# Grouped-query decode attention: a shorter TensorE program, head and exp sums in one matmul, z built on GpSimd

## Chip, cores, metric

One core of a Trainium2 chip. The metric is the device time of one execution in microseconds (us), as the median of several; lower is better.

## The reference

Two tokens (B = 2, one position each) attend over a cache of 32768 positions, with 32 query heads on 8 key/value heads of width 128. A small gated MLP of the same input multiplies the result. Everything is bf16.

```python
def _A_ref(x, k_cache, v_cache, wq, wo):        # x [2,1,512], caches [2,8,32768,128]
    q = (x @ wq) ...                            # 32 heads, 4 to each K/V head
    scores = einsum("bhqd,bhkd->bhqk", q, k) * (Dh ** -0.5)
    p = softmax(scores)
    o = einsum("bhqk,bhkd->bhqd", p, v)
    return o.reshape(B, Sq, Hq * Dh) @ wo
xn = layernorm(x);  s = A(xn);  g = silu(B(xn)) # B: a small MLP, w1 to w4
return x + s * g
```

The caches are 2 x 8 x 32768 x 128 x 2 bytes each, 268.4 MB together, and every byte is used once. There are 16 groups, one for each pair of token and K/V head. Each brings 8.39 MB of K and 8.39 MB of V.

## The kernel before

K and V of a group are loaded by one DMA each. `kbuf` has three slots of half a K, so that the next K can be loaded once the first half of the present one is consumed. `vbuf` has room for one V. VectorE transposes K in 16 pieces into four T buffers. TensorE multiplies them with z (the query heads, shifted), ScalarE takes the exp, VectorE transposes the result to `pt`, and TensorE forms the product with V in `o`. A last step adds the four head slots of `o`, divides by the exp sums and stores the heads' values. Cut to what matters:

```python
# SP: the order of the loads, and what each waits for
for m in range(1, NG):
    sp.wait_ge(p_k, m);  load_k(m)       # first half of K(m-1) has been multiplied
    sp.wait_ge(p_o, m);  load_v(m)       # value product of m-1 is done
# ScalarE, each group
for j in range(4): act.copy(out=z[...], in_=qr[...])
for i in range(2):
    take(act, s_sc);  act.activation(eps_[i], sc[i], Exp, accum_out=rss[i])
take(act, s_o);  act.copy(out=ob, in_=o)
# VectorE, each group
heads(...)        # take(s_x); reciprocal of S; oT * rec * mask; reduce -> oA
for i in range(2):
    for r in range(8): take(s_tf);  dve.transpose(T[...], kbuf[...])
for i in range(2):                       # around each transpose of exp: sel * exp sums -> sms
    take(dve, s_e);  ...;  dve.transpose(pts[h], eps_[i]);  ...
# TensorE, each group
take(s_ob);  for t in range(4): pe.matmul(oT, lhsT=sel_o[t], rhs=ob[t])      # fp32
for i in range(2):
    for r in range(8): take(s_t);  4 matmuls z x T -> sc[i]
    mark(s_tf);  ...                     # 1x1 matmuls, only to raise a semaphore
take(s_p);  pe.matmul(S, lhsT=sms[1], rhs=ones_f[:, 0:1])
64 matmuls pts x vbuf -> o;  mark(p_o)
```

The softmax here doesn't subtract the row's maximum and nothing guards it: scores larger than these inputs give would overflow.

## Time and profile before

| | before |
|---|---|
| time, median of 3 runs | 654.21 us (654.19 to 655.46) |
| span of the profiled execution | 652.8 us |
| bytes read | 280.50 MB |
| TensorE, VectorE, ScalarE, GpSimd busy | 386.2, 346.0, 76.7, 7.7 us |
| TensorE matmul records | 2406 |

"Busy" is the time in which an engine executes. Against it stand the DMA queue's 99.4%, and the time from issue to landing of each load (a load has landed when its last bytes are in the buffer).

### The profile page before, as it was taken

The numbers are of one execution on the slowest core, as the hardware profiler recorded it, in microseconds if no ns is written. First come the engines' busy times: TensorE is split into PE (matmuls) and PEld (weight loads), VectorE is DVE, ScalarE is ACT, GpSimd is POOL, SyncE is SP. The second block draws the span as 40 slices with busy tenths as digits, with TensorE's granted clock in tenths as the row PEclk, the third lists the DMA queues.
The fourth block names the chain that finished last, engine by engine and source line by source line (L and its number), as shares of the span: only waits on it lengthen the run. The fifth ranks groups of instructions, "written<-read, shape, count | busy, mean of one in ns | idle before, by whom it ended". The sixth has DMA issues, their size and how long they took to land. (4 is left out here: it accounts for less than half of the span.)

```text
span 652.8 us, 6524 instructions
## 1 busy us (share of the span) xinstructions
PE 386.2 (59%) x2406; PEld 156.5 (24%) x2438; DVE 346.0 (53%) x412; ACT 76.7 (12%) x184; POOL 7.7 (1%) x29
## 2 busy tenths in 40 slices
PE   0548195672828658293764829367383945828785
PEld 0113132230313213131221213123121322212332
DVE  4257191753809266391835629174481926539570
ACT  1320102020010201101020010201001020010100
POOL 3100000000000000000000000000000000000000
PEclk9769688695978859697786878878697896869798
DMA  9999999999999999999999999999999999999997
GB/s 386 475 396 448 446 446 410 434 446 450 414 426 446 450 422 418 446 450 422 418 446 450 430 410 450 446 438 402 450 446 446 398 446 446 446 406 434 426 442 294
DMA packets 6506, 280.53 MB, mean 430 GB/s; under 512 B 736, under 2 KB 1000, under 8 KB 1256
## 3 DMA queue, kind: packets, MB, share of 16 engines
q1 hardware_dynamic: 6492, 280.50, 99.4%
q8 instruction: 1, 0.02, 0.0%
q10 hardware_dynamic: 12, 0.01, 0.0%
q14 instruction: 1, 0.01, 0.0%
HBM read 280.50 MB, written 0.00 MB: 430 GB/s over the span
## 5 line engine op out<-in xcount | busy, mean ns | idle before, releaser
L585 PE MATMUL bank<-T,z 128*128 128x512 bf16 x992 | 272.6, 422 | 189.7 <-PEq L46 184.9
L512 DVE STREAM_TRANSPOSE T<-kbuf 128x1024 int32<-128x1024 int32 x256 | 290.7, 1211 | 130.5 <-DVEq L46 130.5
L585 PEld LDWEIGHTS bank<-T,z 128*128 128x128 bf16 x1024 | 97.4, 103 | 352.1 <-issue 274.9
L602 PE MATMUL bank<-vbuf,pt 128*16 128x512 bf16 x1024 | 73.0, 449 | 2.5 <-PEq L46 2.5
L489 ACT ACTIVATE ep<-bank 128x512 bf16<-128x512 f32 x32 | 19.1, 598 | 438.5 <-ACTq L46 438.5
L533 DVE RECIPROCAL rec<-bank 128x1 f32<-128x1 f32 (+1 forms) x17 | 2.9, 169 | 118.8 <-DVEq L46 118.8
L602 PEld LDWEIGHTS bank<-vbuf,pt 128*16 128x16 bf16 x1024 | 27.6, 102 | 39.7 <-issue 21.5
L521 DVE STREAM_TRANSPOSE pt<-ep 128x512 bf16<-128x512 bf16 x32 | 22.9, 715 | 22.0 <-DVEq L46 22.0
L567 PE MATMUL bank<-ob,sel_o 128*128 128x128 f32 x136 | 19.7, 289 | 16.4 <-PEq L46 16.4
L595 PE MATMUL bank<-ones_f,sm 128*128 128x1 f32 x32 | 6.2, 264 | 31.3 <-PEq L46 31.3
L567 PEld LDWEIGHTS bank<-ob,sel_o 128*128 128x128 f32 x136 | 16.9, 196 | 21.8 <-issue 21.8
L493 ACT COPY ob<-bank 128x512 f32<-128x512 f32 x16 | 9.4, 587 | 102.6 <-ACTq L46 102.6
L482 ACT ACT_TABLE_LOAD x16 | 20.5, 1283 | 0.3
L595 PEld LDWEIGHTS bank<-ones_f,sm 128*128 128x128 f32 x32 | 5.3, 210 | 32.2 <-issue 32.2
L482 ACT COPY z<-qr 32x16 bf16 x64 | 13.0, 202 | 0.7
L451 PE MATMUL bank<-vbuf,h_bf 128*32 128x512 bf16 x14 | 4.9, 523 | 6.2 <-DVE h_bf L448 6.2
L562 PE MATMUL bank<-ident 128*1 128x1 bf16 x64 | 8.4, 165 | 0.0
L328 PE MATMUL bank<-ident,xn_bf 17*128 17x17 bf16 x4 | 0.3, 177 | 13.1 <-POOL x L319 13.1
L562 PEld LDWEIGHTS bank<-ident 128*1 128x1 bf16 x64 | 4.0, 82 | 16.2 <-issue 14.4
L541 DVE TENSOR_REDUCE oA<-xm 128x128 f32 x16 | 5.9, 366 | 3.8 <-DVEq L46 3.8
L535 DVE SCALAR_TENSOR_TENSOR xm<-bank,rec,mask 128x128 f32<-128x128 f32 (+1 forms) x17 | 6.0, 351 | 2.5 <-DVEq L46 0.2
L489 ACT ACTIVATION_READ_ACCUMULATOR ep<-bank 128x1 f32 x32 | 6.4, 200 | 0.2
(75 smaller groups left out, 55.1 us busy)
## 6 DMA issues: line engine op xcount, KB each, us to landing
vbuf<-in_A_v_cache_dram SPq DMA_DIRECT2D x4, 4096.0 KB, 29.5
kbuf<-in_A_k_cache_dram SPq DMA_DIRECT2D x2, 4096.0 KB, 22.9
kbuf<-in_A_wq_dram SPq DMA_DIRECT2D x1, 4096.0 KB, 13.5
vbuf<-in_B_w_dram SPq DMA_DIRECT2D x2, 1792.0 KB, 18.2
kbuf<-in_A_wo_dram SPq DMA_DIRECT2D x3, 1024.0 KB, 34.4
kbuf<-in_A_wo_dram SPq DMA_DIRECT2D x1, 512.0 KB, 37.1
kbuf<-in_A_wo_dram SPq DMA_DIRECT2D x1, 256.0 KB, 37.3
kbuf<-in_A_wo_dram SPq DMA_DIRECT2D x2, 128.0 KB, 37.1
```

Of the source, the lines that this page charges most:

```text
L482: i = act.copy(out=z[32 * j:32 * j + 32, :, :, c:c + rep], in_=qr[32 * j:32 * j + 32, :, :, bass.ds(m * rep, rep)],)
L489: act.activation(out=eps_[i][:, :], in_=sc[i][:, :], func=ACT.Exp, scale=inv_sqrt_dh, accum_out=rss[i][:, :]).then_inc(s_e, 1)
L493: act.copy(out=ob[:, :], in_=o[:, :]).then_inc(s_ob, 1)
L512: dve.transpose(out=Ts[(NR * i + r) % T_BUFS][:, :].rearrange("p (b t k) -> p t b k", b=NB, t=RT), in_=kt[:, r * W:(r + 1) * W].rearrange( ...
L521: dve.transpose(out=pts[h][:, :, :].rearrange("p r (t h) -> p t r h", h=rep), in_=eps_[i][:, :].rearrange("p (t r h) -> p t r h", r=NR, h= ...
L535: dve.scalar_tensor_tensor(out=xm[p0:, :, :], in0=oT[p0:, :].rearrange("p (w r) -> p w r", w=WL), scalar=rec[p0:, 0:1], in1=mask[p0:, :].u ...
L541: dve.tensor_reduce(out=dst, in_=xm[p0:, :, :].rearrange("p w r -> p r w"), axis=AX.X, op=ALU.add).then_inc(s_r, 1)
L562: pe.matmul(mark_ps, lhsT=ident[:, 0:1], rhs=ident[:, 0:1], start=True, stop=True).then_inc(sem, 1)
L567: mm = pe.matmul(oT, lhsT=sel_o[:, t, :, :, :].rearrange("p j h w -> p (j h w)"), rhs=ob[:, t * Dh:(t + 1) * Dh], start=(t == 0), stop=(t ...
L585: mm = pe.matmul(sc[i][:, :], lhsT=z[:, nb, e, zc:zc + 128], rhs=Tb[:, nb, :, e], start=(r == 0 and nb == 0 and e == 0), stop=(r == NR - 1 ...
L595: pe.matmul(S, lhsT=sms[1][:, :], rhs=ones_f[:, 0:1], start=True, stop=True)
L602: mm = pe.matmul(o[32 * j:32 * j + VT * rep, :], lhsT=pts[h][:, r, a * VT * rep:(a + 1) * VT * rep], rhs=vt[:, u * VT:(u + 1) * VT, :].rea ...
```

## The change

The intent is a TensorE program that is short (446 instructions, as the prediction has it) and less work around each group. The two halves of a group become a TensorE loop with register addresses, and the groups a loop with a counter. The four selection matmuls and the exp-sum matmul become one fp32 matmul of 129 columns. For this VectorE masks `o` and adds its four head slots, and writes the sum of the two exp sums into column 129. The marker matmuls go: ScalarE raises those semaphores, and V now waits for the heads. GpSimd builds z. The prologue is rearranged in the same spirit (transposes on VectorE, one memset of all of PSUM, the MLP's matmuls in loops). At the end, three quarters of the second half of wo also go through the packed product. Core of the diff, with cuts marked:

```diff
-        sp.wait_ge(p_o, m)
+        sp.wait_ge(s_r, m + 1)            # V after the heads of the group before
         load_v(m)
 ...
-    with act.Fori(0, NG) as m:            # z copies, two exps, copy of o
+    with act.Fori(0, NG):
         for i in range(NPART):
             take(act, s_sc)
+            act.sem_inc(s_tl, 1)
+            act.sem_inc(p_k, 1)
+            if i == NPART - 1:
+                act.sem_inc(s_zf, 1)
             act.activation(... Exp ..., accum_out=rss[i]).then_inc(s_e, 1)
-        take(act, s_o)
-        act.copy(out=ob[:, :], in_=o[:, :]).then_inc(s_ob, 1)
+    with pool.Fori(0, NG) as m:
+        take(pool, s_zf)
+        pool.tensor_tensor(out=zw, in0=qr[... m ...], in1=sel_j[...], op=ALU.mult).then_inc(s_z, 1)
 ...
     def heads(dst, p0):
+        take(dve, s_o)
+        then(dve.tensor_tensor(out=ox, in0=o, in1=sel_t (broadcast), op=ALU.mult))
+        dve.tensor_reduce(out=ob[:, 0:Dh], in_=ox as "p d t", op=ALU.add).then_inc(s_ob, 1)
         take(dve, s_x)
-        then(dve.reciprocal(out=rec[p0:, :], in_=S[p0:, :]))
+        then(dve.reciprocal(out=rec[p0:, :], in_=oT[p0:, Dh:]))
 ...
     def head_sums():
         take(pe, s_ob)
-        for t in range(VT):
-            mm = pe.matmul(oT, lhsT=sel_o[:, t, ...], rhs=ob[:, t * Dh:(t + 1) * Dh], ...)
+        mm = pe.matmul(oT, lhsT=sel_h[...], rhs=ob[:, :], start=True, stop=True)
 ...
-        for i in range(NPART):            # written out twice, marks after each
+    with pe.Fori(0, NPART) as i:
             ... pe.matmul(sc2[:, bass.ds(i * 512, 512)], lhsT=z[...], rhs=Tb[...])
-        pe.matmul(S, lhsT=sms[1][:, :], rhs=ones_f[:, 0:1], start=True, stop=True)
```

## The prediction

> **What bounds the kernel now.** I read the page first, for which unit never rests. The DMA row of the slices and the queue table answer it.
>
> ```profile
> DMA  9999999999999999999999999999999999999997
> q1 hardware_dynamic: 6492, 280.50, 99.4%
> q8 instruction: 1, 0.02, 0.0%
> HBM read 280.50 MB, written 0.00 MB: 430 GB/s over the span
> ```
>
> One queue keeps the 16 DMA engines busy for 99.4% of the span; TensorE stands at 59% and VectorE at 53%. So the question is only whether the change can open a hole in that stream, or lengthen what comes before its first byte or after its last. The fetch of instructions is one packet of 0.02 MB. The stretch table, cut into windows of 38.64 us (the distance between two K landings), shows whether the rate wanders. The columns are PE, PEld, DVE, ACT and POOL busy, clock, DMA share, GB/s:
>
> ```profile
> 80.14:118.78 38.64, 23.78 (x140) 9.40 (x142) 20.78 (x24) 4.17 (x10) 0.00 (x0) 0.81 1.00 434
> 311.98:350.62 38.64, 23.80 (x140) 9.45 (x142) 20.79 (x24) 4.18 (x10) 0.00 (x0) 0.81 1.00 434
> 543.82:582.46 38.64, 23.86 (x140) 9.54 (x142) 20.79 (x24) 4.17 (x10) 0.00 (x0) 0.81 1.00 434
> ```
>
> All of the 14 full groups run at 434 or 435 GB/s. A group brings K and V of 8.39 MB each, 16.78 MB, and 16.78 MB / 434 GB/s = 38.66 us: the period is the transfer and nothing else. The single slices of 396 to 450 on the page are whole packets falling on one or the other side of a border. Last, the chain that ended last, which tells what follows the stream:
>
> ```profile
> 613.16 36.97 DMA kbuf<-in_A_wo_dram
> 650.13 0.04 issue
> 650.18 0.26 PE bank L637 x4
> 650.46 0.30 DVE sg L662
> 650.79 0.29 DVE out L664
> ```
>
> The last bytes of wo land at 650.13 us, and only 0.95 us of work follows before the output's DMA is issued. Before the stream there is about 1 us (the first issue is at 0.00).
>
> How much delay can the stream take? A load is issued when its buffer is free, and waits behind the one in flight. The DMA issue view gives the time from issue to landing:
>
> ```profile
> kbuf<-in_A_k_cache_dram SPq DMA_DIRECT2D x15, 27.5
> vbuf<-in_A_v_cache_dram SPq DMA_DIRECT2D x14, 31.4
> ```
>
> A transfer takes 8.39 / 434 = 19.3 us, so a typical K load is issued 27.5 - 19.3 = 8.2 us early and a V load 31.4 - 19.3 = 12.1 us. About 1 us of each is the issue's own latency. That leaves 7 us and 11 us in hand, and all that the change does inside a group has to be held against them.
>
> **What the Trainium skill says.** "DMA: Bandwidth & Descriptors", section "Where 436 GB/s comes from", derives 435 GB/s from the 16 SBUF ports, and expects about 358 from the HBM side for a transfer like this one. The trace shows 434, so here the port figure is the one met, and the HBM figure is not the limit with this one core running. "Runtime: NRT & Kernel Launch", section "Instruction fetch mechanics", says that instructions come in blocks of 256 through a small buffer and that a taken branch out of the buffered window stalls. I take that for the intent of the 446-instruction program. The trace before shows one fetch packet on q8 in the whole span, so there is no stall of that kind to win back. "VectorE: DVE Perf Modes", section "The perf-mode tier table", puts a fp32 tensor_tensor and a tensor_reduce at the slowest mode whatever the memory, which I use for the two new VectorE operations. Before, a 128x128 reduction took 0.366 us and a 512-wide statistics pass 0.69 us, which agrees with about 1 ns per element plus a fixed part of some 0.2 us.
>
> **The change part by part, inside a group.** Tail of group 14 before, from the timeline:
>
> ```profile
> 570.94 0.59 ACT L493 COPY ob<-bank 128x512 f32<-128x512 f32 x1 [6.97 <-ACTq L46]
> 571.67 1.13 PE L567 MATMUL bank<-ob,sel_o 128*128 128x128 f32 x8 [0.86 <-PEq L46]
> 572.95 0.17 DVE L533 RECIPROCAL rec<-bank 128x1 f32<-128x1 f32 x1 [7.89 <-DVEq L46]
> 573.27 0.35 DVE L535 SCALAR_TENSOR_TENSOR xm<-bank,rec,mask 128x128 f32<-128x128 f32 x1
> 573.85 0.37 DVE L541 TENSOR_REDUCE oA<-xm 128x128 f32 x1 [0.24 <-DVEq L46]
> 582.42 18.14 DVE L512 STREAM_TRANSPOSE T<-kbuf 128x1024 int32<-128x1024 int32 x16 [8.20 <-DVEq L46]
> ```
>
> VectorE finishes group 14's heads at 574.2 and stands still for 8.20 us until the next K has landed.
>
> - Removed: the 0.59 us copy on ScalarE, 1.13 us of matmuls on TensorE, two scalar operations on VectorE of 0.26 and 0.31 us, the exp-sum matmul (0.35 us), four marker matmuls per group, and on ScalarE the z copies (0.85 us) with their 1.28 us table load.
> - Added on VectorE: the mask over 128x512 from PSUM (estimate 0.65 us), the sum of four over 512 elements (estimate 0.72 us), a one-element add (0.15 us); on TensorE one fp32 matmul of 129 columns (2 of the 8 passes above, about 0.4 us with its latency); on GpSimd one small product for z, which starts when the second half's scores are done and has some 19 us until the next K lands.
> - VectorE's own time per group: + 0.65 + 0.72 + 0.15 - 0.26 - 0.31 = + 0.95 us, on 20.8 us in 38.64.
> - From the end of the value matmuls (570.8) to the end of the heads: before 3.4 us; after about 0.1 + 0.65 + 0.15 + 0.72 + 0.1 + 0.4 + 0.1 + the same 1.25 us (reciprocal to reduction) = 3.5 us. Before the value product it saves about 0.7 us (exp sums). VectorE's idle 8.20 us therefore stays near 8 us, and K loads, issued after the first half's scores, move by nothing.
> - Moved: the V load waits for the end of the heads and no longer for the value matmuls. V is issued 3.5 us later, of 11 us in hand: about 7.5 us remain. The T buffers are handed back in the same order. The TensorE loop adds a branch per half and per group; even 1 us each would fit.
>
> So 15 groups by 0 us is 0 us.
>
> **Start.** The stream before V's held-back half of group 0 is 4.19 (wq) + 3.67 (w3, w4) + 8.39 (K) + 4.19 (V) = 20.4 MB, 47 us at 434 GB/s, and in fact K landed only at 41.5, so until about 51. The half waits for the w4 product, which ended at 31.8. After, the tanh need no longer queue behind 12 ScalarE copies (about 3 us sooner), but the w3 product is no longer packed (16 matmuls one after another, 3 us for 1.2), hT takes four transposes for one (+1.5 us), and two loops add branches: I put the end of w4 at 33 to 38 us. That is 13 us before it matters. VectorE was ready for K at 37.9; I expect 40 to 44, perhaps 2 us past the landing at 41.5. That delays the K load of group 1, but it was issued at 52.57 and is needed by about 60 (41.5 + 19.3, less 1). Hidden, with about 5 us to spare. First DMA issue: unchanged.
>
> **End.** The wo parts land in sequence; the matmuls before waited for data at 647.7, 648.85, 649.53, 649.86 and 650.17. After, the fourth part (landing 648.85) also goes through the four-way packed product, the ScalarE copy (0.59 us) and the fp32 selection (0.40 us): 648.85 + 0.35 + 0.05 + 0.59 + 0.05 + 0.40 = 650.3, just past the last landing at 650.17, and then eight small matmuls. I charge + 0.2 us. The heads of the last group end near 646.4 (before 646.75), ahead of the third part at 647.7.
>
> Sum: 654.21 + 0 + 0 + 0.2 = 654.4 us.
>
> **Rivals.**
> 1. *The later V issue opens a hole.* For: it is the one load that now sits behind a chain of five dependent steps. Against: 11 us in hand. A chain of 8 us more than before would be needed; if it were 12 us, 4 us x 15 = 60 us, some 714.
> 2. *Branches on TensorE cost a fetch each.* For: the skill's warning, with DMA queues full of 64 KB packets. If each half stalled for 3 us, score work of 20 us would become 26 us, K loads move by 3 us or V by 6, still inside 7.5; only beyond that would the period grow, by 1 us each for 16 us in all (670). Against: the program before already loops over all 16 groups with a single packet fetched.
> 3. *The removal helps: less TensorE and ScalarE work, some per cent faster.* Against: their idle time is already the larger part of a group, and the stream is full. Nothing to win beyond the 0.95 us after the last byte and 3 us of slow start.
> 4. *The prologue opens a hole* (loops or 16 GpSimd copies slower than thought, so that group 1's K comes late): 1 to 6 us, at most 660.
>
> **Range and chances.** The three runs before spread from 654.19 to 655.46, and my one non-zero term is 0.2 us, so 653.7 to 655.8. Two per cent is 13 us: faster would need fewer bytes or a higher rate, slower would need rival 1 or 2 at full size. Faster 0.005, slower 0.02, the rest within.
>
> **What would show it.** Right: DMA row of nines again, 434 GB/s in every group window, q1 at 280.50 MB, K still about 27 us from issue to landing, V about 28 (31.4 - 3.5), VectorE idle before the first K transposes near 8 us a group, the chain ending in wo's DMA. VectorE busy near 346 + 15 = 361 us, TensorE instructions down by some 240 of 2406. Wrong: V to landing under 21 us, a digit below 9 in the DMA row, more than one or two packets on the instruction queues, or a chain that runs through VectorE or TensorE for most of a group.

## More of the kernel before

A load that waits in the queue behind another has been issued early, and how early is the margin that a slower compute chain may use up before the time changes.

## The result, and the profile after

The changed kernel takes 654.41 us (median of 6 runs, 653.9 to 655.44) against 654.46 us for the kernel before (6 runs, 654.19 to 655.46). The ratio is 1.0, with a 95% interval of 0.9987 to 1.0012: the same. Ratios in this document are the mean time of one kernel's fast runs over that of the other's of the same rounds, so not quite the ratio of the medians.

| | before | after |
|---|---|---|
| TensorE, VectorE busy, us | 386.2, 346.0 | 376.6, 375.5 |
| ScalarE, GpSimd busy, us | 76.7, 7.7 | 49.4, 11.9 |
| TensorE matmul records | 2406 | 2164 |
| bytes read, MB | 280.50 | 280.50 |

The page of the changed kernel, its DMA rows and its queue:

```profile
DMA  9989998999899989998999899989998999899997
GB/s 387 482 386 450 450 450 386 450 450 450 386 450 450 446 390 450 450 450 386 450 450 450 386 450 450 450 386 450 450 450 386 450 450 450 386 450 420 447 420 322
q1 hardware_dynamic: 6492, 280.50, 99.5%
```

The same bytes fill the same 16 DMA engines. The eights in the DMA row look like small holes and are none. A round of packets is 16 x 64 KB = 1.05 MB, and in a slice of 652.4 / 40 = 16.3 us that is 64.3 GB/s. The page counts a packet where it starts, so a slice has six rounds (386) or seven (450), depending on where the border falls. Cut by whole group periods (from one K landing to the next), the rate is what it was, as in one of the stretches that the prediction also showed:

```profile
543.82:582.46 38.64, 21.90 (x128) 8.49 (x130) 22.21 (x25) 2.66 (x5) 0.29 (x1) 0.77 1.00 434
```

The issues of the loads, with the median time to landing:

```profile
kbuf<-in_A_k_cache_dram SPq DMA_DIRECT2D x15, 27.2
vbuf<-in_A_v_cache_dram SPq DMA_DIRECT2D x14, 27.3
```

K is issued as early as before (27.5), V 4.1 us later (31.4), and it still lands in time. The tail of the group that the prediction showed, from the timeline:

```profile
568.49 0.69 DVE L502 TENSOR_TENSOR ox<-ps,sel_t 128x512 f32<-128x512 f32 x1 [4.09 <-DVEq L46]
569.32 1.02 DVE L507 TENSOR_REDUCE ob<-ox 128x128 f32<-128x512 f32 x1
570.49 0.67 PE L543 MATMUL ps<-ob,sel_h 128*128 128x129 f32 x2 [2.16 <-PEq L46]
...
572.21 0.36 DVE L519 TENSOR_REDUCE oA<-xm 128x128 f32 x1 [0.24 <-DVEq L46]
572.60 0.33 SPq L226 DMA_DIRECT2D vbuf<-in_A_v_cache_dram  x1
581.53 18.14 DVE L486 STREAM_TRANSPOSE T<-kbuf 128x1024 int32<-128x1024 int32 x16 [8.96 <-DVEq L46]
```

The V load is issued 0.03 us after the heads' last operation, and VectorE then stands still for 8.96 us until the next K has landed. That is not to be held against the 8.20 us of before: the value product of this group took 3.63 us here and 5.32 there. The group before it, with 5.32 us, leaves 7.60 us. The end of the chain that ended last:

```profile
648.83 0.59 ACT T L629
...
649.47 0.41 PE ps L633 x8
...
650.36 0.29 DVE out L643
```

The last bytes of wo landed at 649.43 us, while the ScalarE copy ran; the selection follows, as the prediction's term for the end said. This chain, and no longer wo's landing, leads to the output. From wo's landing to the issue of the output's DMA it is 650.68 - 649.43 = 1.25 us, before 651.11 - 650.13 = 0.98. The stream itself ended 0.70 us earlier, and it had started so: the first K landed at 40.19 us, before at 41.26 (39.99 to 40.35 in the profiles of all variants of the changed kernel, 41.26 to 41.46 in those of the kernel before). Nobody forecast that, and its cause is open. The spans of single executions differ by as much (652.2 to 653.1 over six runs of the changed kernel).

### The profile page after: what moved, and what is told of

It reads as the page before. It is cut to its first block, busy times and chain, and to the rows that moved or that the text cites. A ratio compares the mean times of both kernels' runs of the same rounds, so it can differ in the third digit from the quotient of the medians.

```text
span 652.4 us, 6348 instructions
## 1 busy us (share of the span) xinstructions
PE 376.6 (58%) x2164; PEld 140.1 (21%) x2196; DVE 375.5 (58%) x430; ACT 49.4 (8%) x92; POOL 11.9 (2%) x45
## 3 DMA queue, kind: packets, MB, share of 16 engines
q1 hardware_dynamic: 6492, 280.50, 99.5%
HBM read 280.50 MB, written 0.00 MB: 430 GB/s over the span
## 5 line engine op out<-in xcount | busy, mean ns | idle before, releaser
L566 PE MATMUL ps<-T,zeros 128*128 128x512 bf16 x992 | 276.5, 425 | 173.2 <-PEq L46 164.4
L566 PEld LDWEIGHTS ps<-T,zeros 128*128 128x128 bf16 x1024 | 98.8, 104 | 346.1 <-issue 267.8
L579 PE MATMUL ps<-vbuf,pt 128*16 128x512 bf16 x1024 | 71.3, 441 | 40.5 <-PEq L46 40.5
L502 DVE TENSOR_TENSOR ox<-ps,sel_t 128x512 f32<-128x512 f32 x17 | 11.8, 692 | 83.4 <-DVEq L46 83.4
L579 PEld LDWEIGHTS ps<-vbuf,pt 128*16 128x16 bf16 x1024 | 29.8, 101 | 82.1 <-issue 65.2
L543 PE MATMUL ps<-ob,sel_h 128*128 128x129 f32 x34 | 9.0, 350 | 39.3 <-PEq L46 39.3
L453 ACT ACTIVATE ep<-ps 128x512 bf16<-128x512 f32 x32 | 19.1, 597 | 104.7 <-ACTq L46 104.5
L507 DVE TENSOR_REDUCE ob<-ox 128x128 f32<-128x512 f32 x17 | 17.3, 1018 | 2.5
L417 PE MATMUL ps<-vbuf,zeros 128*32 x12 | 7.0, 585 | 0.8 <-issue 0.3
L453 ACT ACTIVATION_READ_ACCUMULATOR ep<-ps 128x1 f32 x32 | 6.2, 194 | 0.0
```

Source lines behind the costliest of these rows:

```text
L417: pe.matmul(h2[0:32, :], lhsT=h_bf[:, bass.ds(f, 1), :].rearrange("p f c -> p (f c)"), rhs=w4v[:, bass.ds(f, 1), :].rearrange("p f d -> p ...
L453: act.activation(out=eps_[i][:, :], in_=sc[i][:, :], func=ACT.Exp, scale=inv_sqrt_dh, accum_out=rss[i][:, :]).then_inc(s_e, 1)
L502: dve.tensor_tensor(out=ox[:, :].rearrange("p (t d) -> p t d", t=VT), in0=o[:, :].rearrange("p (t d) -> p t d", t=VT), in1=sel_t[:, :].uns ...
L507: dve.tensor_reduce(out=ob[:, 0:Dh], in_=ox[:, :].rearrange("p (t d) -> p d t", t=VT), axis=AX.X, op=ALU.add).then_inc(s_ob, 1)
L543: mm = pe.matmul(oT, lhsT=sel_h[:, :, :, :].rearrange("p j h w -> p (j h w)"), rhs=ob[:, :], start=True, stop=True)
L566: mm = pe.matmul(sc2[:, bass.ds(i * 512, 512)], lhsT=z[:, nb, e, zc:zc + 128], rhs=Tb[:, nb, :, e], start=(r == 0 and nb == 0 and e == 0), ...
```

## The experiments

The theory: the byte stream sets the time of both kernels, and all that the change does on the engines is hidden under it, within a margin. The rivals: what the change removes and adds cancels on the chain; V's later issue already costs; the program's length or its branches cost or gain. Every experiment ran beside the kernel before, on the same chip; the rounds ran on four chips (1 to 4, 5 to 7, 8 to 10, 11 and 12). Groups are counted from 0 here.

**1 and 2. Half the bytes, in both kernels.** If the stream is cut below the compute chain, the chain itself becomes visible. For groups 2 to 14 only half of each K and V buffer is loaded; the other half keeps old data. The result is wrong, although the comparison with the reference still passed.

```diff
-        if m < last:
-            sp.dma_start(out=dst, in_=row_view(cache, *groups[m])).then_inc(sems[0], 16)
+        if 2 <= m < last:
+            w = slice(0, 2 * SLOT * 1 // 2)
+            sp.dma_start(out=dst[:, w], in_=row_view(cache, *groups[m])[:, w]).then_inc(sems[0], 16)
+        elif m < last:
+            ...                            # as before
```

> The kernel before with the K and V loads of groups 2 to 14 cut to half their bytes (13 x 8.39 MB = 109 MB less; the other half of each buffer keeps old data, so the result is wrong on purpose). My theory (the byte stream sets the time, and a compute chain of about 30.3 us a group lies hidden under its 38.6 us): groups 2 to 14 now run at the chain's own pace, transposes 18.1 + exp, value product, heads = 30.3 us as seen once in the trace before where K was already there (582.42 to 612.70); in all about 537 us. Rival 'cancel' (the chain itself binds or is equally long in both kernels): no difference between this run and its partner. Rival 'bytes alone' (nothing but bytes ever counts): 654 - 109/0.434 = 403 us.

Measured: 535.64 us, ratio 0.8191 (0.8177 to 0.8205). The compute chain of the kernel before is hidden under the stream, at 30.3 us a group, as read from its trace.

> The changed kernel with the same cut. My theory: the chain of the changed kernel is about 29.3 us a group (581.53 to 610.84 in its trace), 1.0 us shorter, so about 13 us less than the partner: near 524 us, 2 to 3% faster than it. Then the change did buy compute time, and the full stream hides it. Rival 'cancel' (what was removed and what was added on the chain are equal): the two within 0.5%. Rival 'bytes alone': 403 us, both the same.

Measured: 548.05 us, ratio 0.8367 (0.8348 to 0.8387). The theory of the bytes holds, since this kernel too runs a good 100 us faster. My claim of a chain that is 1.0 us shorter falls: it is longer, 12.4 us in all. The two timelines show where. Group 8 of the kernel before, which begins its transposes at 289.06:

```profile
310.74 5.32 PE L605 MATMUL bank<-vbuf,pt 128*16 128x512 bf16 x64
...
316.19 0.59 ACT L496 COPY ob<-bank 128x512 f32<-128x512 f32 x1 [6.97 <-ACTq L46]
...
316.92 1.13 PE L570 MATMUL bank<-ob,sel_o 128*128 128x128 f32 x8 [0.86 <-PEq L46]
...
319.10 0.37 DVE L544 TENSOR_REDUCE oA<-xm 128x128 f32 x1 [0.24 <-DVEq L46]
319.38 18.13 DVE L515 STREAM_TRANSPOSE T<-kbuf 128x1024 int32<-128x1024 int32 x16
```

Group 8 of the changed kernel, which begins at 295.23:

```profile
316.80 5.32 PE L582 MATMUL ps<-vbuf,pt 128*16 128x512 bf16 x64 [2.23 <-PEq L46]
322.28 0.69 DVE L505 TENSOR_TENSOR ox<-ps,sel_t 128x512 f32<-128x512 f32 x1 [5.77 <-DVEq L46]
323.12 1.02 DVE L510 TENSOR_REDUCE ob<-ox 128x128 f32<-128x512 f32 x1
324.28 0.46 PE L546 MATMUL ps<-ob,sel_h 128*128 128x129 f32 x2 [2.16 <-PEq L46]
...
326.07 18.13 DVE L489 STREAM_TRANSPOSE T<-kbuf 128x1024 int32<-128x1024 int32 x16
```

From the first transpose to the value product it is 21.68 us before and 21.57 after. From the end of the value product (start plus 5.32) to the next transposes it is 3.32 before and 3.95 after. A group is 30.32 us before and 30.84 after. So 0.1 us is gained ahead of the value product and 0.63 lost behind it. The longest of the new steps is the sum over four slots, 1.02 us.

That is some 0.5 us x 14 = 7 us of the 12.4. The remainder is in the value product: in the kernel before it took about 3.6 us instead of 5.3 in four of the groups, as here in group 12, in the changed kernel in none.

```profile
432.01 3.63 PE L605 MATMUL bank<-vbuf,pt 128*16 128x512 bf16 x64
```

Three of the four count (the first still waits for a full-size load): such a group lasts 28.63 us, and 3 x 1.69 is 5.1 us. Experiments 8 to 12 take this up. My 29.31 us came from a group whose value product happened to be a fast one.

**3 and 4. V held back by about 14 us, in both kernels.** SP asks the idle GpSimd, which runs 12 chained memsets before the V load is issued. In the changed kernel:

```diff
         sp.wait_ge(s_r, m + 1)
+        sp.sem_inc(s_q, 1)
+        sp.wait_ge(s_g, m + 1)
         load_v(m)
 ...                                       # GpSimd, after building z
+        take(pool, s_q)
+        for _ in range(12):
+            pool.memset(scratch[:, :], 0.0).then_inc(s_w, 1)
+            take(pool, s_w)
+        pool.sem_inc(s_g, 1)
```

> The kernel before, with each V load held back by 12 chained memsets on the idle GpSimd (about 14 us, an estimate from 1.31 us for 1456 elements plus a 0.24 us step). My theory: V has about 11 to 13 us in hand, so a small hole opens of 1 to 2 us a group (a later V also lands later and makes the next K later, which halves the hole): 662 to 685 us. Rival 'the delay counts in full': 654 + 15 x 14 = 860 us. Rival 'V is never near the path': 654 us.

Measured: 692.02 us, ratio 1.0571 (1.0553 to 1.0588).

> The changed kernel with the same delay of about 14 us on each V load. My theory: here V had only 8 us in hand, so the hole is larger, near 3.8 us a group once it has settled (late V delays the value product, which delays the next V): 695 to 720 us, some 25 to 40 us over the partner. That would show that the change spent headroom and not time. Rival 'the delay counts in full': 860 us. Rival 'headroom is the same in both': equal to the partner.

Measured: 753.43 us, ratio 1.1507 (1.1488 to 1.1526).

Both are above my ranges; the order and the sign are as expected, and the rivals "in full" (860), "never" (654) and "the same headroom in both" fall. The size missed because of what a load costs when the stream has run dry. In both kernels the line of the V loads reads

```profile
vbuf<-in_A_v_cache_dram SPq DMA_DIRECT2D x14, 21.8
```

which is 2.5 us over the pure transfer of 19.3, where I had put 1. The Trainium skill has it: "DMA: Bandwidth & Descriptors", section "Latency and other measured facts", speaks of a fixed cost of about 2 us per DMA; here it is 2.5. With it the period can be worked out as a loop, from one V landing to the next. Before: value product 5.3, hand-over and delay 13.5, issue to landing 21.8, together 40.6; the K loads were issued 40.95 us apart. After: value product 4.9 to 6.6, heads 4.0, hand-over and delay 13.5, 21.8, together 44.2 to 45.9; measured 45.2. So the change has put the 4.0 us of heads into the loop that returns the V buffer. Without a delay the loop is about 27.4 us before and 31.4 after, under the transfer period of 38.64 in both.

**5. V held back by 4 memsets, changed kernel only.** The edit is that of experiment 4 with 4 in place of 12.

> The changed kernel with each V load held back by 4 memsets on GpSimd (4.5 us from the step of 1.10 us that the longer delay showed). The loop of one V load is now worked out from the runs with 12 memsets: landing, value product 5.3, heads 4.0, issue to landing 21.8 in an empty stream, 0.5 of hand-over, that is 31.6 us without a delay, against a transfer period of 38.64. With 4.5 us it is 36.1 us, still under the period: 654 us, within 0.3% of the kernel before, V loads issued 4.5 us later. Rival 'every us of V delay costs': 654 + 15 x 4.5 = 721 us.

Measured: 661.83 us, ratio 1.0121 (1.0092 to 1.015). A miss: small, but clear of the noise. The rival of 721 us falls as well, so most of the delay is hidden and not all. The lines:

```profile
vbuf<-in_A_v_cache_dram SPq DMA_DIRECT2D x14, 23.4
119.39:158.60 39.21, 21.96 (x128) 8.58 (x130) 22.20 (x25) 2.66 (x5) 4.10 (x5) 0.76 1.00 428
```

The V loads now land 23.4 us after issue, 1.6 us over the 21.8 of an empty stream, as a median. Those behind a slow value product (1.7 us later) land after 21.8 to 23.3. The loss is uneven: the single periods of K run from 38.64 to 40.42 us. Nor is 21.8 a sharp edge: the V load issued at 310.93 us landed after 23.22 us, and that was still 20.51 us after the K before it, where the pure transfer is 19.3. In this stretch the engines still count as busy (1.00) while the rate is 428 GB/s: part of the loss is packets that take longer, not only empty time. So the margin has to be counted from 21.8 at least, and not from 19.3 plus 1: the changed kernel has at most 27.3 - 21.8 = 5.5 us at the median, the kernel before 31.4 - 21.8 = 9.6. I had expected some 7.5 and 11. What the last 1 or 2 us above 21.8 cost, and why, stays open.

**6 and 7. Seven eighths of the bytes, in both kernels.** The edit of experiment 1 with `7 // 8`.

> The kernel before with K and V of groups 2 to 14 at seven eighths of their bytes (wrong result on purpose). Transfer period 33.8 us, still over the compute chain of about 30.0 us that the half-byte run showed: only the bytes count, 27.26 MB less at 0.434 MB/us = 62.8 us less: 591.5 us.

Measured: 591.77 us, ratio 0.9045 (0.903 to 0.906). To the microsecond what the bytes alone give.

> The changed kernel with the same cut. Its chain is about 30.8 us and its V loop about 31.6 minus 2.4 for the shorter transfer, both under 33.8: 591.5 us as well, within 0.4% of the partner. If the changed kernel had a hidden cost that already binds at the full size, it would be slower here, by up to 0.8 us x 13 = 11 us (1.8%).

Measured: 596.05 us, ratio 0.9136 (0.9094 to 0.9179). It misses the bytes' figure by 4.3 us. Two groups of its trace:

```profile
217.37:252.64 35.27, 22.57 (x128) 7.98 (x130) 22.08 (x24) 2.66 (x5) 0.29 (x1) 0.84 0.99 421
286.54:320.34 33.80, 21.59 (x128) 8.25 (x130) 22.20 (x24) 2.66 (x5) 0.29 (x1) 0.85 1.00 434
```

Most groups run at the transfer's 33.8 us; some are up to 1.5 us longer, with a lower rate. This fits experiment 5: a period shorter by 38.64 - 33.80 = 4.84 us takes that much from the margin of 5.5 us, as the 4 memsets did there with 4.6 us (from the end of the heads to V's issue, by the trace), and both lose. At the full size nothing is lost: the periods of the changed kernel are 38.6 to 38.7 us throughout.

**8 to 10. What makes the changed chain longer? Half the bytes, one part undone in each.** First the sum of four is done by matmuls again; then the TensorE loop over halves is written out; then the base once more on the same chip.

```diff
 # half_nosum
-        dve.tensor_reduce(out=ob[:, 0:Dh], in_=ox ..., op=ALU.add).then_inc(s_ob, 1)
+        pe.matmul(oT[:, Dh:], lhsT=sel, rhs=ob[:, Dh:], start=True, stop=True)
+        for t in range(VT):
+            mm = pe.matmul(oT[:, 0:Dh], lhsT=sel, rhs=ox[:, t * Dh:(t + 1) * Dh], start=(t == 0), stop=(t == VT - 1))
 # half_unroll
-    with pe.Fori(0, NPART) as i:
+    for i in range(NPART):                 # and sc[i] in place of the register address
```

> The changed kernel with half the K and V bytes, and with the VectorE sum over the four head slots (1.02 us) taken out: four accumulating matmuls add the four masked blocks instead (1.28 us to the reciprocal, as in the kernel before), and one column for the exp sums. Correct sums, half the data. If the added VectorE sum is what makes the changed chain longer: reciprocal about 0.4 us earlier in each group, 15 groups: about 542 us, against 548.05 for the changed kernel with half the bytes. Rival 'the TensorE loop and its branches do it': no change, 548 us.

Measured: 546.02 us, ratio 0.8349 (0.8335 to 0.8363).

> The changed kernel with half the K and V bytes, its TensorE loop over the two halves of a group written out (two copies, constant addresses; the loop over groups stays). If the branch and the register-addressed matmuls cost: the second exp comes 0.2 us earlier as in the kernel before (19.47 instead of 19.69 us after the first transpose), 15 x 0.2 = 3 us: 545 us. If the program's length mattered (longer again: 64 more score matmuls less the loop), it would be slower than 548 us, with more instruction packets.

Measured: 546.16 us, ratio 0.8343 (0.8329 to 0.8357).

> The changed kernel with half the bytes once more, on this chip, as the base for the two others: 548 us again, within 0.3%.

Measured: 546.41 us, ratio 0.8355 (0.8337 to 0.8372). All three are the same within their intervals, so removing the sum did not bring the gain expected of it, nor did the written-out loop. Writing the loop out changes nothing, down to the time of the second exp's transpose (it ends 21.23 us after the first transpose, as in the base), so the branch of this loop (32 matmuls a pass) and its register addresses cost nothing that can be seen here. The branch once a group stayed in and was not tested. Taking the sum off VectorE shortened the heads by 0.27 us (3.88 to 3.61 from mask to end), but the group's period only went from mostly 30.72 to mostly 30.57: the value product took 5.32 us instead of 5.19. Something else holds the period.

**11 and 12. Keeping TensorE's clock up.** The period of the base and of the written-out version is 30.72 us in group after group, and TensorE's clock gives a hint. The windows around the value product in two groups that follow each other (from experiment 2; the seventh number from the left counts the clock, between GpSimd's busy time and the DMA share):

```profile
313.50:316.91 3.41, 1.17 (x8) 0.44 (x12) 1.21 (x3) 0.69 (x2) 0.29 (x1) 1.00 1.02 442
316.91:320.32 3.41, 3.41 (x36) 1.38 (x32) 0.00 (x0) 0.00 (x0) 0.00 (x0) 0.50 0.00 0
...
347.63:351.04 3.41, 3.39 (x36) 1.22 (x40) 0.00 (x0) 0.00 (x0) 0.00 (x0) 0.50 0.00 0
```

A stretch of 3.41 us at half clock begins at 316.91 and again at 347.63, 30.72 us later, each after a window in which TensorE was little busy (1.17 and 1.14 of 3.41 us). The Trainium skill, "TensorE: Matmul & The Clock Gate", section "What's actually happening", describes a window of 3413 ns that runs freely and by whose activity the clock is halved or released; 30.72 us is nine such windows, and the records of this trace begin and end on that grid. The value product, which comes after a 2.2 us wait for the exp, therefore runs at half clock for most of its time in every group of this trace. That the period settles on the grid can be watched in experiment 10, here the value products of groups 2, 4 and 8, at periods of 30.84, 30.78 and 30.72 us:

```profile
130.25 5.32 PE L582 MATMUL ps<-vbuf,pt 128*16 128x512 bf16 x64 [2.23 <-PEq L46]
191.93 5.24 PE L582 MATMUL ps<-vbuf,pt 128*16 128x512 bf16 x64 [2.23 <-PEq L46]
314.92 5.19 PE L582 MATMUL ps<-vbuf,pt 128*16 128x512 bf16 x64 [2.23 <-PEq L46]
```

At 30.84 us the half-clock stretch comes 0.12 us earlier in each group, from 0.13 us after the product's start (group 2) to 0.21 us before it (group 8). Less of the product then lies in it, the group gets shorter, and at nine windows it stays. With the sum by matmuls (experiment 8) the period of 30.57 us is 0.15 short of nine windows. The stretch moves the other way through the product, from 0.06 us after its start (group 2) to 1.25 (group 14), and only group 15 is fast. In the kernel before, at 30.32 us, it moves 0.40 us a group, and after 1.10, 0.98 and 1.26 us (groups 2, 6 and 11) the next product is fast: this is where its fast value products come from. (These places are taken from the clock records of the traces.)

Eight filler matmuls in TensorE's wait should undo it:

```diff
+    for _ in range(8):
+        pe.matmul(banks[5], lhsT=ident, rhs=ident.unsqueeze(1).to_broadcast([128, 4, 128]), start=True, stop=True)
     take(pe, s_p)
```

> The changed kernel with half the K and V bytes, and eight filler matmuls on TensorE (an unused PSUM bank) after each group's scores, where it otherwise waits 2.2 us for the exp and its transpose. Theory 'clock window': in the half-byte runs the group period of the changed kernel sits at 30.72 us, nine times the 3.413 us of which the clock records are multiples, so each value product falls into the same half-clock window and takes 5.3 us; kept busy, TensorE gets the full clock and the product takes 3.7 us, as in 4 of 16 groups of the kernel before. Period near 29.1 us, total near 522 us, below the 535.6 of the kernel before with half the bytes. Rival 'the chain's added steps alone make the 10 us': the fillers take nothing away, 546 us or a little over.

Measured: 528.27 us, ratio 0.8074 (0.8061 to 0.8088), some 18 us less than without the fillers, and 7 us less than the kernel before at half its bytes (both from other rounds; by the ratios to the kernel before it is the same). The period is 29.16 us in most groups, as expected; the total is 6 us above my figure. The clock and the value product now:

```profile
306.60:310.30 3.70, 3.63 (x64) 1.63 (x64) 0.00 (x0) 0.00 (x0) 0.00 (x0) 1.00 0.31 133
```

All 64 matmuls in 3.63 us at full clock. The rival, that the added steps alone make the difference, falls. But they make the larger part of the 12.4 us of experiments 1 and 2, about 7, and the clock about 5: with a fast value product in both kernels a group is 29.16 us against 28.63, still 0.53 longer. The kernel before was not run with fillers.

The last run adds two shortenings, the matmul sum of experiment 8 and this:

```diff
             take(act, s_sc)
-            act.sem_inc(s_tl, 1) ...       # three increments ahead of the exp
             act.activation(... Exp ...).then_inc(s_e, 1)
+            act.sem_inc(s_tl, 1) ...       # behind it
```

> The same with two steps shortened: the three semaphore increments of ScalarE behind the exp instead of ahead of it (the second exp came 0.22 us later than in the kernel before), and the sum of four done by matmuls instead of VectorE (it took 0.27 us off the heads, but the period did not follow). If the lock to the clock window swallowed those gains before, they show now: 0.5 us a group less, about 515 us. Rival 'they are worth nothing': equal to half_warm.

Measured: 522.33 us, ratio 0.7977 (0.7964 to 0.7991), 5.9 us less than experiment 11; my total of 515 was again 7 us too low. The period is 28.67 us in seven of thirteen groups, 0.49 less than 29.16 and within 0.04 of the kernel before's 28.63, and the transposes of the exp end at 21.01 us instead of 21.23, so 0.22 us of it is the three increments. So the sum of four and the increments account for 0.49 of the 0.53 us. The same matmul sum that gave 0.15 us a group at half clock gives its 0.27 once the clock is full. The increments alone at half clock were not tried.

None of these variants can beat either kernel at full size, where the stream sets 38.64 us a group and the chain is 8 us shorter, so none was run as a candidate.

## Why the prediction was right

1. *The stream sets the time: right.* The periods of groups 1 to 13 are 38.6 to 38.7 us, at 434 GB/s, in both kernels. With seven eighths of the bytes the kernel before needs 591.77 us where the bytes say 591.5.
2. *Nothing inside a group reaches the stream: right, with less room than stated.* The step "about 1 us of each is the issue's own latency" was too small: it is 2.5 us (21.8 - 19.3). The margin of V is at most 5.5 us and not 7.5, and experiments 5 and 7, which take 4.6 and 4.8 us from it, already cost 7.6 and 4.3 us.
3. *The heads take about as long as before (3.4 to 3.5 us), and the value product starts 0.7 us earlier: wrong, without effect.* Measured at half the bytes: 3.32 to 3.95 behind the value product, and 0.1 us gained ahead of it. Behind it the sum of four was the term furthest off (0.72 estimated, 1.02 measured); small gaps make up the rest. Ahead of it the exp sums gave 0.33 us and not 0.7 (the gap between the exp's last transpose and the value product went from 0.67 to 0.34), and the three increments ahead of the exp took 0.22 of that. In sum a group is 0.5 us longer instead of 0.6 shorter, and at half the bytes its value product is slow more often. The table load on ScalarE, which the prediction counted as removed, is still there (16 loads of 1.28 us on both pages); it now stands before the first exp, off the chain.
4. *V is issued later: right.* 31.4 - 27.3 = 4.1 us, forecast 3.5. K's issue did not move (27.5 and 27.2).
5. *The start: right.* The w4 product ended at 35.7 (forecast 33 to 38), the first K transposes began at 42.57 (40 to 44), and group 1's K was issued at 53.70, where about 60 was the limit by my count. Not foreseen: the first loads landed 1.1 us earlier, so the estimate was right partly by luck. And the w4 product, now a loop with one matmul a pass, took 8.60 us instead of 4.87 (mean clock 0.54 and 0.65). Loop and clock were not tried apart; all of it is hidden.
6. *The end: + 0.2 us, right in the trace, too small to show in the times.* From wo's landing to the output it is 0.27 us more (1.25 and 0.98). The chain at the end runs as the sum said, through the copy and the selection. The sign that I named for it was wrong: I wrote that the chain would end in wo's DMA.
7. *The rivals.* V's later issue (rival 1) and the branches (rival 2) cost no time at full size. (The page before has a second instruction packet, on q14, which the prediction passed over; the page after has that one alone.) Fewer instructions gained nothing (rival 3), and the prologue opened no hole (rival 4).
8. *Other signs.* TensorE's records fell by 242 (forecast 240). VectorE's busy time rose by 29.5 us and not by 15: about 22 of it is per-group work (17.3 for the sums, 11.8 for the masks, 1.9 for the one-element adds, less 9.1 for what went), the rest mostly the prologue, among it one memset of PSUM. "A digit below 9 in the DMA row" was a bad sign, since it depends on where slice borders fall.

## What to carry to other kernels

When one queue is full, work out how early each load is issued, counted from its landing time in an empty stream and not from size over rate; changes to the engines matter only against that margin. A change that "does nothing" can still spend it: here V's margin went from 9.6 to 5.5 us at the most, and a 12% shorter transfer already shows it. To see what a change does to a hidden compute chain, cut the bytes until the chain is bare, and look at the TensorE clock before crediting a shorter or longer step.

## What the Trainium skill lacked or had wrong

- "DMA: Bandwidth & Descriptors", section "Where 436 GB/s comes from": the sentence that the HBM side, about 358 GB/s, binds for transfers from HBM to SBUF lacks its condition. One core alone held 434 GB/s through 14 groups here. The same page says elsewhere that 358 is each core's part when both cores of a domain stream, so the page isn't wrong as a whole.
- The same page has no figure for how far ahead a load must be queued so that the stream stays full. Here 27.3 us from issue to landing (median) lost nothing, 23.4 lost 7.6 us over 15 loads, unevenly, and the pure transfer is 19.3.
- "TensorE: Matmul & The Clock Gate" describes the free-running window, but not that a loop can lock to it: at half the bytes the period went from 30.84 to 30.72 us (nine windows) and stayed there, also with the loop written out. A shortening worth 0.27 us a group gave 0.15 before the clock was kept up.
- No page has the time of a tensor_reduce over a strided inner dimension. "VectorE: DVE Perf Modes", section "The perf-mode tier table", puts it at the same slowest mode as an fp32 tensor_tensor, and for 512 fp32 elements the product took 0.69 us, the sum of four 1.02. "SBUF — State Buffer" says that strided accesses pay, without a figure for VectorE. Stride and reduction were not tried apart.
- No page has what a semaphore increment costs on ScalarE ahead of a waiting instruction: three of them delayed the exp by 0.22 us.
